# Gated infini-attention on one core: O weighed in 32-token blocks turned by VectorE, memory by quads of heads, products copied out of PSUM once

## The chip, the core and the metric

The kernel runs on one core of a Trainium2 chip. TensorE (PE in the profile) multiplies matrices into PSUM, which has eight banks of 128 x 512 floats. VectorE (DVE), ScalarE (ACT) and GpSimd (POOL) work on tiles of 128 partitions; GpSimd reads and writes SBUF only. SyncE (SP) issues every DMA. The metric is device time in microseconds (us); the kernel before has a median of 1042.45 us over 3 runs (1041.78 to 1042.59).

## The reference

There are two branches, A and B, each with its own weights, on the same x of 2048 tokens by 640 features. Each has 32 heads of 20 features and goes through 4 segments of 512 tokens in turn. In a segment, with S the causal softmax and g = sigmoid(beta) per head:

```python
a_dot = softmax(q @ k.T * scale + mask) @ v
a_mem = (phi(q) @ M) / (phi(q) @ z + 1e-6)      # phi(t) = t + 1 if t > 0 else exp(t)
o     = g * a_mem + (1 - g) * a_dot
M, z  = M + phi(k).T @ v, z + phi(k).sum()      # memory, carried to the next segment
```

A branch's output is o @ wo, and the result is s * A + (1 - s) * B with s = sigmoid(x . gate_w) per token. Everything is float32.

## The kernel before

The work is laid out by a planner in Python: the function keeps a clock of its own for every engine (queues `A`, `D`, `G` and `S` for ScalarE, VectorE, GpSimd and SyncE), gives each operation an estimated cost, and emits the instructions in the order in which its clock reaches them. Each engine then runs its own list in that fixed order, and waits on semaphores. The costs, the table `RULES` and the priorities therefore set the order on every engine, and a changed cost anywhere moves instructions everywhere.

There are 8 stages `t` (4 segments, A and B in turn), and in each 8 units `u` of 4 heads (a quad), so 64 units `i = 8 t + u`. TensorE's array is used as two halves of 64 rows, called lanes here, that run side by side; only PV (below) takes the whole array, in four column strips.

- Products (`job_qk`, `job_v`, `job_o`, line 643): x @ wq, wk, wv and O @ wo. Each operand is split into a high and a low part (fp32r), and three products are added, 15 matmuls of 512 columns in each lane. The products are the fill that keeps TensorE occupied between the units' steps.
- A finished q or k product is read out of its PSUM bank by `hi_lo_out` (ScalarE makes the high part, line 628, VectorE the low one, line 612) and by `hi_lo_phi` (lines 595 to 606), which makes phi; the bank is free when all have read it. High and low parts go to DRAM (`qd`, `kd`) and come back as quads (`qst`, `kst`, line 1032).
- S (line 1074) computes scores for the row maxima, which VectorE takes (line 1061, two instructions each); T (line 1164) computes the transposed scores, ScalarE the exponentials (line 1156), GpSimd the causal mask (line 1157).
- PV (line 1184) multiplies with v, which lies in `vst`, one tile for each branch, with a column of ones per head for the sum. Its result has 32 partitions per head (20 values, the sum, 11 that are not used) and 512 tokens.
- `fin_unit`: the result is copied out (line 1209), turned back to tokens on partitions by 8 matmuls with the identity (`turn`, line 790), weighed by VectorE (lines 1248 to 1250) into `ft` or O, and added to O by GpSimd (line 1259).
- `mem_unit` (line 752) multiplies phi(q) with the memory `mbd` into tokens on partitions, for 19 or 13 heads at a time, and VectorE weighs it into O (lines 766 to 769). `back_unit` and `update_unit` (lines 790, 830, 851) renew the memory.
- `o_transpose` turns O once more (8 matmuls, line 790), and ScalarE and VectorE split it (line 1277) for the product with wo.

## Time and profile before

| | before |
|---|---|
| median of 3 runs | 1042.45 us |
| the profiled execution's span, first to last instruction | 1041.1 us (no other time of this execution is given; the median is 1.3 us more) |
| TensorE busy, instructions | 1031.4 us (99%), 11778 |
| VectorE busy | 759.5 us (73%) |
| ScalarE busy | 663.7 us (64%) |
| GpSimd busy | 583.9 us (56%) |
| DMA, mean share of 16 engines | 65% |
| granted TensorE clock | 1.00 |

Busy time is the union of the instructions' spans. A matmul's span holds its way through the array too, so that matmuls overlap and the distance between two starts says what one of them costs. A float32 matmul stands in the trace as two matmuls, each with its weight load (PEld); an fp32r matmul or a turn with the identity stands as one.

### The profile page before, as it was taken

The page shows a single profiled execution, that of the slowest core. Times are in us where ns is not written, and L with a number is a line of the kernel's source. Part 1 is how long each engine was busy: PE and PEld are TensorE (multiplying, and loading weights), DVE is VectorE, ACT ScalarE, POOL GpSimd, SP SyncE. Part 2 cuts the span into 40 slices and gives each one's busy share as a digit, 9 for nine tenths or more (in the row PEclk, how much of TensorE's full clock was granted, in tenths as well). Part 3 has the DMA queues.
Part 4 walks back from the last instruction along what each step waited for, and adds up shares of the span by engine and source line. Part 5 has one row for each costly group of instructions (what it writes and reads, how often), then busy time and mean ns, then how long its engine had stood idle before and what let it go on. Part 6 is the DMA issues. An engine that isn't in the chain of part 4 may idle for free.

```text
span 1041.1 us, 31911 instructions
## 1 busy us (share of the span) xinstructions
PE 1031.4 (99%) x11778; PEld 875.0 (84%) x11778; DVE 759.5 (73%) x2714; ACT 663.7 (64%) x1346; POOL 583.9 (56%) x1045
## 2 busy tenths in 40 slices
PE   9999999999999999999999999999999999999998
PEld 7887798888988889887898988988879888787876
DVE  4797877668776688776877768877578767788763
ACT  6376667667664576565857558666675756766581
...
GB/s 270 309 277 166 204 244 221 189 176 258 150 229 130 199 267 181 223 160 160 271 154 227 129 215 251 200 212 155 203 250 156 256 157 195 265 159 225 127 118 52
DMA packets 110027, 207.96 MB, mean 200 GB/s; under 512 B 12464, under 2 KB 16560, under 8 KB 109872
## 3 DMA queue, kind: packets, MB, share of 16 engines
...
## 4 chain that ended last, share of the span: by engine, by line
PE 94%; DMA 3%; ACT 1%; DVE 1%; SPq 0%; POOL 0%; issue 0%; ACTq 0%; DVEq 0%
PE bank L643 54%; PE bank L1184 14%; PE bank L1164 7%; PE bank L1074 7%; PE bank L790 4%; PE bank L830 3%; PE bank L752 3%; DMA kst<-kd 1%; DMA row<-in_xT_dram 1%; DMA wst<-in_a_wk_dram 1%; PE bank L691 1%; PE bank L1099 0%; DMA qd<-row 0%; PE bank L1003 0%; DVE row L988 0%
## 5 line engine op out<-in xcount | busy, mean ns | idle before, releaser
L1061 DVE CUSTOM_DVE_ANT_0 bank<-bank,tri 128x384 f32<-128x384 f32 (+3 forms) x1024 | 474.8, 518 | 163.3 <-PE bank L1074 137.6
L643 PE MATMUL bank<-row,wh 64*128 64x512 f32 x2308 | 518.4, 404 | 0.3
L1156 ACT ACTIVATE p<-bank 128x512 f32<-128x512 f32 x598 | 328.6, 599 | 143.2 <-PE bank L1164 104.9
L1157 POOL TENSOR_SCALAR_AFFINE_SELECT p<-p 128x256 f32<-128x256 f32 (+1 forms) x598 | 214.3, 367 | 264.2 <-ACT p L1156 251.6
L643 PEld LDWEIGHTS bank<-row,wh 64*128 64x128 f32 x2308 | 322.9, 185 | 14.6 <-issue 1.8
L643 PE MATMUL bank<-row,wl 64*128 64x512 f32 x1154 | 302.4, 400 | 0.0
L472 POOL TENSOR_TENSOR wl<-wst,wh 128x640 fp32r<-128x640 f32 x115 | 181.6, 1582 | 46.5 <-ACT wh L470 46.0
L643 PE MATMUL bank<-wvh,row 64*128 64x320 f32 x1280 | 192.7, 318 | 0.1
L643 PEld LDWEIGHTS bank<-row,wl 64*128 64x128 f32 x1154 | 173.6, 185 | 6.4 <-issue 1.4
L1074 PE MATMUL bank<-kst,qst 60*128 60x128 f32 (+3 forms) x1024 | 176.9, 320 | 2.0 <-DMA kst<-kd 1.3
L1164 PE MATMUL bank<-qst,kst 62*128 62x128 f32 (+3 forms) x1024 | 174.6, 318 | 0.0
L643 PEld LDWEIGHTS bank<-wvh,row 64*128 64x128 f32 x1280 | 153.4, 185 | 3.1 <-issue 1.6
L1184 PE MATMUL bank<-p,vst 128*32 128x512 f32 (+3 forms) x1948 | 145.3, 431 | 0.0
L1061 DVE DVE_READ_ACCUMULATOR2_ANT mx<- 128x1 f32 x1024 | 143.3, 140 | 0.0
L1164 PEld LDWEIGHTS bank<-qst,kst 62*128 62x128 f32 x1024 | 126.9, 186 | 8.8 <-issue 1.4
L1074 PEld LDWEIGHTS bank<-kst,qst 60*128 60x128 f32 x1024 | 125.3, 185 | 10.6 <-issue 3.0
L1184 PEld LDWEIGHTS bank<-p,vst 128*32 128x32 f32 x1948 | 58.3, 109 | 85.6 <-issue 63.6
L643 PE MATMUL bank<-wvl,row 64*128 64x320 f32 x640 | 107.9, 312 | 0.0
L470 ACT CAST wh<-wst 128x640 fp32r<-128x640 f32 x119 | 86.5, 736 | 19.0 <-PE bank L643 13.0
L1209 ACT COPY row<-bank 128x512 f32<-128x512 f32 x62 | 36.5, 588 | 79.0 <-PE bank L1184 74.4
L643 PEld LDWEIGHTS bank<-wvl,row 64*128 64x128 f32 x640 | 85.6, 185 | 0.4 <-issue 0.4
L790 PE MATMUL bank<-ident,row 64*128 64x64 f32 x752 | 75.4, 225 | 0.5 <-DVE mx L1061 0.2
...
## 6 DMA issues: line engine op xcount, KB each, us to landing
qd<-row SPq DMA_DIRECT2D x120, 256.0 KB
kd<-row SPq DMA_DIRECT2D x120, 256.0 KB
qst<-qd SPq DMA_DIRECT2D x128, 240.0 KB
kst<-kd SPq DMA_DIRECT2D x128, 240.0 KB
...
```

What stands on the lines that cost most here:

```text
L470: put("A", 0.66, lambda: nc.scalar.copy(wh, w3), lambda: put(lo_eng, lo_cost, lambda: lo.tensor_tensor(out=wl, in0=w3, in1=r32(wh), op=ALU ...
L472: lambda: lo.tensor_tensor(out=wl, in0=w3, in1=r32(wh), op=ALU.subtract), end, prio=3), prio=6)
L643: return nc.tensor.matmul(bank_of, lhsT=w[ROWS[half]], rhs=x_[ROWS[half]], start=start, stop=stop)
L752: return nc.tensor.matmul(pm[:, a - h0:c - h0, :].rearrange("p h e -> p (h e)"), lhsT=r32(pqTs[t, m][ROWS[half], P * n:P * (n + 1)]), rhs= ...
L790: return nc.tensor.transpose(px[:, n, r], block(n)[r], ident[r, r])
L1061: put("D", w / 960.0 + 0.112, lambda: nc.vector.tensor_tensor_reduce(out=sc[:, off:off + w], in0=sc[:, off:off + w], in1=tri[:, L - w:], s ...
L1074: lane_ops[half].append((w * 0.000458, lambda pair=pair, qb=qb, off=off, w=w, r=r, sc=sc: nc.tensor.matmul(sc[:, off:off + w], lhsT=q[r, p ...
L1156: put("A", 0.49, lambda: nc.scalar.activation(pt, sc, AF.Exp, scale=SCALE), lambda: (bank.give(sc), put("G", 0.05 + 0.16 * len(todo), lamb ...
L1157: "G", 0.05 + 0.16 * len(todo), lambda: nc.gpsimd.affine_select(out=blocks, in_=blocks, pattern=[[0, len(todo)], [1, P]], base=0, channel_ ...
L1164: lane_ops[half].append((w * 0.000458, lambda pair=pair, kb=kb, off=off, w=w, r=r, sc=sc: nc.tensor.matmul(sc[:, off:off + w], lhsT=k[r, p ...
L1184: nc.tensor.matmul(po[32 * j:32 * j + 32, P * kb:], lhsT=vst[t % 2][:, kb, h * E1:h * E1 + 32], rhs=pts[i, n, f][0][:, off:off + w], start ...
L1209: either(0.52, lambda: nc.scalar.copy(r32(oT), po), 0.63, lambda: nc.vector.tensor_copy(r32(oT), po), end, 2)
```

## The change

- PV's result (and the memory's) is no longer turned on TensorE. VectorE turns it from its bank into a row in blocks of 32 x 32 (`weighed`, line 944 of the changed kernel): 32 tokens of a block come to lie on partitions, and each head keeps its group of 32 partitions, so that a partition holds a head's tokens in 16 blocks. The weights are worked out there (lines 862 to 866), and the row is scaled straight into O's tile (`scale`, line 888), or scaled in place and then added (`scale_own`, `add`, lines 891 and 896), by VectorE or GpSimd, whichever the planner's cost prefers, with 0.6 us put on VectorE's side.
- O's tiles `Z[t, k]` hold 32 features of a head group; `o_turn` (line 962) turns each back by VectorE. The features thereby come in another order, and wo's rows are put in that order at the start by `relay`: 13 DMAs for each branch within DRAM, in three steps (`nat`, `lin`, `wop`, lines 480, 473, 468). The loads of wo read `wop`.
- `mem_unit` takes a quad at a time with the memory as the stationary operand and phi(q) as the moving one, 512 columns wide (line 837), in place of the pieces of 84, 63 and 21 columns. `mall`, one tile for each branch, replaces `mbds`.
- A q or k product is copied out of its bank once (line 749, ScalarE or VectorE), and the bank is free; high, low and phi are made from the row in SBUF (lines 675, 692, 701 to 718), the low part by VectorE or GpSimd.
- One `vst` serves both branches, and `job_v` waits for the PV and the updates of the stage before. The rows that are shared (`NBIG`) go from 27 to 42.
- The token gates are spread to the new layout (line 621, 64 copies of 32 x 4), the planner's cost model has other costs, and `RULES` other numbers.

```diff
--- before.py
+++ after.py
-        0: "TSTSTSTSTS 1.010 2.38 0.30 8",
-        2: "TTSTSTSTSS 1.023 2.38 0.30 8",
...
+        0: "TSTSTSTSTS 1.036 3.71 0.31 6",
+        1: "TSTSTSTSTS 1.0 2.38 0.33 6",
+        2: "TSTSTSTSTS 1.0 2.38 0.36 6",
...
-    DONE = {"A": 0.14, "D": 0.11, "G": 0.1, "S": 0.0}
+    DONE = {"A": 0.14, "D": 0.12, "G": 0.1, "S": 0.0}
+    SEEN, MAX_DONE = 0.127, 0.06
...
-        e = min(ways, key=lambda e: load[e] + ways[e][0])
+        e = min(ways, key=lambda e: load[e] + ways[e][0] + 0.6 * (e == "D"))
...
-    mbds = [[const.tile([P, HI[m] - LO[m] + 1, E1], F32, name=f"mbd{b}_{m}") for m in range(KT)] for b in range(2)]
+    mall = [const.tile([P, H, 32], F32, name=f"mall{b}") for b in range(2)]
...
-    vst = [const.tile([P, NB, H * E1 + 12], F32, name=f"vst{i}") for i in range(2)]
+    vst = const.tile([P, NB, H * E1 + 12], F32, name="vst")
...
+    nat = [dram.tile([D, D], F32, name=f"nat{b}") for b in range(2)]
+    lin = [dram.tile([4, 8 * DH, D], F32, name=f"lin{b}") for b in range(2)]
+    wop = [dram.tile([P, KT, D], F32, name=f"wop{b}") for b in range(2)]
-    NBIG, NWST, NWH, SPARE = 27, 4, 4, 2
+    NBIG, NWST, NWH, SPARE = 42, 4, 4, 2
...
+    def relay(b):
...
+        def third(j):
+            dma(1.2, lambda: nc.sync.dma_start(
+                out=wop[b][32 * j:32 * j + 32], in_=lin[b][j].rearrange("(k q) c -> q k c", k=KT)), last, prio=RELAY[b])
+        def second():
+            for j in range(4):
+                dma(1.2, lambda j=j: nc.sync.dma_start(
+                    out=lin[b][j].rearrange("(u e) c -> u e c", e=DH),
+                    in_=nat[b].rearrange("(u j e) c -> j u e c", u=8, j=4)[j]), lambda j=j: third(j), prio=RELAY[b])
+        last = then_all(4, there)
+        first = then_all(KT, second)
+        for m in range(KT):
+            dma(1.2, lambda m=m: nc.sync.dma_start(
+                out=nat[b][:, P * m:P * (m + 1)].rearrange("(k p) c -> p k c", p=P), in_=weights[b]["o"][m]), first, prio=RELAY[b])
+    RELAY = (150.0, 260.0)
...
+            def fetch():
+                src_ = src[m] if kind in "qk" else wop[t % 2][:, :, P * m:P * (m + 1)]
+                dma(0.84, lambda: nc.sync.dma_start(out=w3, in_=src_), landed, prio=0 if i < 4 else need[i])
...
-            put("D", 0.63, lambda: nc.vector.tensor_tensor(out=lo, in0=src, in1=r32(hi), op=ALU.subtract), out, prio=1)
+            anyof(1, out, D=(0.65, lambda: nc.vector.tensor_tensor(out=lo, in0=r32(raw), in1=r32(hi), op=ALU.subtract)),
+                  G=(1.255, lambda: nc.gpsimd.tensor_tensor(out=lo, in0=r32(raw), in1=r32(hi), op=ALU.subtract)))
...
+    def phi_out(raw, y, read):
+        def end():
+            big.give(raw)
+            read[1](y)
+        def least():
+            put("D", 0.35, lambda: nc.vector.tensor_scalar(raw, raw, 0.0, 1.0, op0=ALU.max, op1=ALU.add), lambda: put(
+                "D", 0.65, lambda: nc.vector.tensor_tensor(out=y, in0=raw, in1=y, op=ALU.min), end, prio=1), prio=1)
+        def most():
+            put("D", 0.65, lambda: nc.vector.scalar_tensor_tensor(
+                out=y, in0=raw, scalar=0.0, in1=y, op0=ALU.max, op1=ALU.add), end, prio=1)
+        def summed():
+            put("D", 0.35, lambda: nc.vector.tensor_scalar(raw, raw, 0.0, None, op0=ALU.max), lambda: put(
+                "G", 1.255, lambda: nc.gpsimd.tensor_tensor(out=y, in0=raw, in1=y, op=ALU.add), end, prio=1), prio=1)
+        if load["D"] < load["A"]:
+            both = then_all(2, least)
+            put("A", 0.535, lambda: nc.scalar.activation(y, raw, AF.Exp), both, prio=2)
+        else:
+            both = then_all(2, summed if load["G"] + 0.9 < load["D"] else most)
+            put("A", 0.535, lambda: nc.scalar.activation(y, raw, AF.Relu, scale=-1.0), lambda: put(
+                "A", 0.535, lambda: nc.scalar.activation(y, y, AF.Exp, scale=-1.0), both, prio=2), prio=2)
+        read[0].append(both)
...
+            big.want((F32,), lambda raw: either(
+                0.478, lambda: nc.scalar.copy(raw, pp), 0.6, lambda: nc.vector.tensor_copy(raw, pp), lambda: out(raw), 1), prio=1)
...
+    def mem_unit(t, u):
+        w = mall[t % 2][:, 4 * u:4 * u + 4, :].rearrange("p h e -> p (h e)")
+        half_m = [next(c // 2 for c in CHUNKS[u] if c % 2 == half) for half in range(2)]
+        def mm(half, start, stop):
+            r = ROWS[half]
+            return nc.tensor.matmul(b, lhsT=w[r], rhs=r32(pqTs[t, half_m[half]][r, :]), start=start, stop=stop)
+        ops = [[(cost_f(L), lambda z0, z1, half=half: mm(half, z0, z1))] for half in range(2)]
...
+        def take():
+            read()
+            big.want((F32,), lambda z: weighed(t, u, b, z, 1), prio=1)
+        return split_unit(*ops, take)
+    def weighed(t, u, b, z, which):
+        z4 = z.rearrange("p (a e) -> p a e", e=32)
+        first = which == 1 or t < 2
+        def weight():
+            w = sb.tile([P, 16], F32, tag="fw", name=f"fw{which}_{t}_{u}", bufs=4)
+            if which:
+                nc.vector.scalar_tensor_tensor(
+                    out=w, in0=z4[:, :, DH], scalar=1e-6, in1=gq[t][1][:, u, :], op0=ALU.add, op1=ALU.mult)
+            else:
+                nc.vector.tensor_tensor(out=w, in0=z4[:, :, DH], in1=gq[t][0][:, u, :], op=ALU.mult)
+            nc.vector.reciprocal(w, w)
+            return w
...
+        def scale(e, w):
+            wb = w[:, :, None].to_broadcast([P, 16, DH])
+            for k, e0, e1 in ZP[u]:
+                dst = Z[t, k].rearrange("p (a e) -> p a e", e=32)[:, :, DH * u + e0 - 32 * k:DH * u + e1 - 32 * k]
+                e.tensor_tensor(out=dst, in0=z4[:, :, e0:e1], in1=wb[:, :, e0:e1], op=ALU.mult)
+        def scale_own(e, w):
+            e.tensor_tensor(out=z4[:, :, :DH], in0=z4[:, :, :DH], in1=w[:, :, None].to_broadcast([P, 16, DH]), op=ALU.mult)
+        def add(e):
+            for k, e0, e1 in ZP[u]:
+                dst = Z[t, k].rearrange("p (a e) -> p a e", e=32)[:, :, DH * u + e0 - 32 * k:DH * u + e1 - 32 * k]
+                e.tensor_tensor(out=dst, in0=dst, in1=z4[:, :, e0:e1], op=ALU.add)
...
+        n = len(ZP[u])
+        D1, G1 = 0.1 * n + 0.33, 0.14 * n + 0.69
+        def turned():
+            bank.give(b)
+            when_gates(lambda: put("D", 0.33, lambda: got_w.append(weight()), lambda: when_placed(go), prio=2))
...
+        def go():
+            w = got_w[0]
+            if first:
+                pair(D1, G1, lambda e: scale(e, w), end, 3)
+            else:
+                pair(0.43, 0.83, lambda e: scale_own(e, w), plus, 3)
+        def plus():
+            if (t, u) in mem_done:
+                pair(D1, G1, add, end, 3)
+            else:
+                at(clk[0] + 0.2, plus)
+        def pair(d, g, fn, then, prio):
+            anyof(prio, then, D=(d, lambda: fn(nc.vector)), G=(g, lambda: fn(nc.gpsimd)))
+        places(lambda: None)
+        put("D", 0.62, lambda: nc.vector.transpose(out=z, in_=b), turned, prio=2)
+    def o_turn(t, k, o):
+        def turned():
+            big.give(Z.pop((t, k)))
+            big.want((F32R, F32R), halves, prio=2)
+        def halves(hi, lo):
+            def end():
+                big.give(o)
+                OTs[t, k] = (hi, lo)
+            put("A", 0.535, lambda: nc.scalar.copy(hi, o), lambda: anyof(
+                2, end, **{x: (c, lambda e=e: e.tensor_tensor(out=lo, in0=o, in1=r32(hi), op=ALU.subtract))
+                           for x, c, e in (("D", 0.65, nc.vector), ("G", 1.255, nc.gpsimd))}), prio=2)
+        z = Z[t, k]
+        put("D", 0.6, lambda: nc.vector.transpose(out=o, in_=z), turned, prio=2)
...
-        yield from hold_on(lambda: t < 2 or oTs_begun[t - 2] == 8 and all((t - 2, m) in upd_done for m in range(KT)), "v")
+        ms = range(KT) if half else range(3)
+        yield from hold_on(lambda: t < 1 or oTs_begun[t - 1] >= 4 + 4 * half and (
+            t > 6 or all((t - 1, m) in upd_done for m in ms)), "v")
...
-    def fin_unit(i):
...
-        def weigh(dst):
-            w = sb.tile([P, NB, 4], F32, tag="fw", name=f"fw{i}", bufs=2)
-            wb = w[:, :, :, None].to_broadcast([P, NB, 4, DH])
-            nc.vector.tensor_tensor(out=w, in0=px[:, :, :, DH], in1=gq[t][0][:, :, 4 * u:4 * u + 4], op=ALU.mult)
-            nc.vector.reciprocal(w, w)
-            nc.vector.tensor_tensor(out=dst, in0=px[:, :, :, :DH], in1=wb, op=ALU.mult)
...
-    def o_transpose(t, k):
...
+        after_whole(lambda: (read(), big.want((F32,), lambda z: weighed(t, u, po, z, 0), prio=1)))
...
+        if (t, kind, m) == (0, "v", 4):
+            relay(0)
+        if (t, kind, m) == (1, "v", 0):
+            relay(1)
```

Three places show how instructions move. On TensorE, behind the PV of unit 27 (`row_8905_8142` is the copied PV result, `mt` the maxima), before:

```order
L1099 MATMUL bank_122<-ident,mt_8067 32x64
L790 MATMUL bank_121<-ident,row_8905_8142 128x64 x3
L643 MATMUL bank_123<-row_8310_7607,wh_135 128x512
L790 MATMUL bank_121<-ident,row_8905_8142 128x64
L643 MATMUL bank_124<-row_8156_7488,wh_129 128x512
L643 MATMUL bank_123<-row_8314_7610,wh_135 128x512
L643 MATMUL bank_124<-row_8305_7604,wh_129 128x512
L790 MATMUL bank_121<-ident,row_8905_8142 128x64 x2
```

and in the changed kernel behind the same PV:

```order
L1275 MATMUL bank_120<-ident,mt_7936 32x64
L734 MATMUL bank_118<-row_8641_7086,wl_128 128x512
L734 MATMUL bank_121<-row_8951_7381,wh_129 128x512
L734 MATMUL bank_118<-row_8682_7140,wl_128 128x512
L734 MATMUL bank_121<-row_8616_7055,wl_130 128x512
L1275 MATMUL bank_120<-ident,mt_7936 32x64
L734 MATMUL bank_118<-row_8804_7245,wl_128 128x512
L1250 MATMUL bank_116<-kst_78,qst_74 128x512
```

The turns with the identity (line 790) are gone, and products and the next S stand in their place. The memory of stage 2 on TensorE (`row` is phi(q)), before and then changed:

```order
L752 MATMUL bank_124<-mbd_0_70,row_4156_3815 128x84
L752 MATMUL bank_120<-mbd_0_70,row_4156_3815 128x84
L752 MATMUL bank_124<-mbd_1_71,row_4341_3960 128x84
L752 MATMUL bank_120<-mbd_1_71,row_4341_3960 128x84
L752 MATMUL bank_124<-mbd_2_72,row_4625_4184 128x84
L643 MATMUL bank_118<-wvh,row_3105_2827 128x320
```

```order
L837 MATMUL bank_120<-row_4601_3820,mall_70 128x512
L837 MATMUL bank_115<-row_4787_3955,mall_70 128x512
L734 MATMUL bank_116<-row_3384_2797,wh_133 128x512
L734 MATMUL bank_116<-row_3389_2800,wh_133 128x512
L837 MATMUL bank_115<-row_4787_3955,mall_70 128x512
L837 MATMUL bank_120<-row_4787_3955,mall_70 128x512
```

Many narrow matmuls with phi(q) as the weights become two wide ones for each quad, one in each lane. On VectorE, around the weighing of unit 23, before and then changed:

```order
L595 TENSOR_SCALAR bank_122<-bank_122 128x512
L1248 TENSOR_TENSOR fw_7123<-bank_121,gqd_140 128x16
L1249 RECIPROCAL fw_7123<-fw_7123 128x16
L1250 TENSOR_TENSOR ft_150<-bank_121,fw_7123 128x320
L596 TENSOR_TENSOR row_7733_7063<-bank_122,row_7733_7063 128x512
L1061 ISA bank_124,mx_7117<-bank_124,tri 128x512
```

```order
L709 TENSOR_SCALAR row_8237_6791<-row_8237_6791 128x512
L944 STREAM_TRANSPOSE row_8391_6900<-bank_121 128x512
L1237 ISA bank_115,mx_6869<-bank_115,tri 128x512
L1237 ISA mx_6869 128x1
L865 TENSOR_TENSOR fw_2_7_6917<-row_8391_6900,gqd_138 128x16
L866 RECIPROCAL fw_2_7_6917<-fw_2_7_6917 128x16
L1237 ISA bank_120,mx_6869<-bank_120,tri 128x512
L1237 ISA mx_6869 128x1
L891 TENSOR_TENSOR row_8391_6900<-row_8391_6900,fw_2_7_6917 128x16x20
L1237 ISA bank_115,mx_6869<-bank_115,tri 128x384
L1237 ISA mx_6869 128x1
L896 TENSOR_TENSOR row_6545_5419<-row_6545_5419,row_8391_6900 128x16x20
```

The weighing read a bank (lines 1248 to 1250); now a block turn reads it (line 944), and the weights, the scaling (line 891) and the addition to O (line 896, on GpSimd at line 1259 before) work on rows in SBUF, each with two operands there. In other units the planner gives the scaling or the addition to GpSimd. The maxima (line 1237, line 1061 before) stand between these steps. On SP, in stage 0 of the changed kernel (before, the rows of lines 480, 473 and 468 aren't there, and the others follow each other):

```order
L480 DMA nat_109<-in_a_wo_dram 128x5x128
L1208 DMA qst_74<-qd_89 60x2x512 x2
L1208 DMA kst_78<-kd_97 60x2x512 x2
L473 DMA lin_111<-nat_109 8x12800 x4
L1287 DMA qst_72<-mr_144 2x8x128 x2
L521 DMA wst_126<-in_b_wv_dram 128x640
L521 DMA wst_123<-in_b_wv_dram 128x640
L468 DMA wop_113<-lin_111 160x1x640 x3
L1208 DMA qst_75<-qd_89 60x2x512 x2
L689 DMA kd_98<-row_1895_1671 128x512 x2
```

The second step (line 473) waits until `nat` has landed, and the third (line 468) for `lin`; the loads of the next quads and the stores of `kd` stand behind them.

More of the change, by code (lines that the diff above doesn't have):

```diff
@@ L1201, in read @@
                         own_p.append(j)
-        def got(oT):
-            def end():
-                bank.give(po)
-                oTs[i] = oT
-                later(1, 0.44, lambda: fin_ok(i), lambda: fin_unit(i))
-            either(0.52, lambda: nc.scalar.copy(r32(oT), po), 0.63, lambda: nc.vector.tensor_copy(r32(oT), po), end, 2)
-        if i % 8 == 0 and t < 2:
-            Ot[t] = None
-            O_store.want(1, lambda o: Ot.__setitem__(t, o), prio=t)
-        after_whole(lambda: (read(), big.want((F32,), got, prio=1)))
```

450 lines of the change are left out of this document (212 added, 238 removed).

## The prediction

> **What bounds the kernel now.** I read the page's busy times first, then the chain of waits over the middle of the run (60 to 980 us), then who waits for whom.
>
> ```profile
> span 1041.1 us, 31911 instructions
> PE 1031.4 (99%) x11778; PEld 875.0 (84%) x11778; DVE 759.5 (73%) x2714; ACT 663.7 (64%) x1346; POOL 583.9 (56%) x1045
> ...
> by line: PE bank L643 57.9%; PE bank L1184 14.7%; PE bank L1074 7.8%; PE bank L1164 7.7%; PE bank L790 4.3%; PE bank L830 3.4%; PE bank L752 3.4%; PE bank L1099 0.5%; issue 0.2%; ACT p L1156 0.1%; DVE bank L1061 0.0%; DVE mx L1061 0.0%; ACT
> ...
> L1061 DVE CUSTOM_DVE_ANT_0 bank<-bank,tri 128x384 f32<-128x384 f32 (+3 forms) x1024 | 474.8, 518 | 163.3 <-PE bank L1074 137.6
> ```
>
> In those 920 us the chain lies on TensorE for 99.7%, and VectorE's longest wait is for TensorE (137.6 us). So TensorE's work sets the time, and a change is worth what it takes from TensorE's lanes, less what new lateness of others makes TensorE wait. How much lateness can be borne two stretches show:
>
> ```profile
> 60.00:70.00 10.00, 10.00 (x119) 8.01 (x119) 9.39 (x34) 8.73 (x20) 8.20 (x15) 1.00 0.97 341
> 120.00:130.00 10.00, 10.00 (x110) 7.95 (x110) 9.52 (x31) 7.32 (x16) 6.28 (x11) 1.00 0.49 165
> ```
>
> The columns are stretch, length, then busy time of PE, PEld, DVE, ACT, POOL, granted clock, DMA share and GB/s. VectorE is busy 94% and 95%, and TensorE still the whole 10 us.
>
> **TensorE: turns removed.** The order has 1072 turns with the identity before and 240 after: 832 go (512 of `fin_unit`, 320 of `o_transpose`).
>
> ```profile
> 60.00:980.00 920.00, 97.54 (x972) 83.04 (x972) 1.00 0.66 200
> ...
> 508.00 0.40 PE L790 MATMUL bank<-ident,row 64*128 64x64 f32 x4
> 508.20 0.39 PE L643 MATMUL bank<-row,wh 64*128 64x512 f32 x1
> 508.24 0.41 PE L790 MATMUL bank<-ident,row 64*128 64x64 f32 x4
> ```
>
> The first row is line 790 alone (972 of its matmuls). Bare, four turns take 0.24 us of one lane (508.00 to 508.24) while the other lane goes on: 0.03 us of both lanes each, 25 us for 832. By the chain it is 4.3% of 920 us over 972, so 40.7 ns, 34 us. The product behind a short turn has too little time to load its weights, and that loss stands on the product's line. So I fitted the 229 stretches of 4 us from 60 to 980 us by least squares: 4 us equals the sum over kinds of count times price. The first and the last of them, all engines and then line 790 alone:
>
> ```profile
> 60.00:64.00 4.00, 4.00 (x45) 3.84 (x45) 3.86 (x20) 3.51 (x8) 3.68 (x6) 1.00 0.96 331
> 976.00:980.00 4.00, 4.00 (x44) 4.00 (x42) 3.86 (x17) 3.72 (x7) 2.96 (x5) 1.00 0.37 108
> ...
> 60.00:64.00 4.00, 0.56 (x4) 0.37 (x4) 1.00 0.96 331
> 976.00:980.00 4.00, 0.00 (x0) 0.00 (x0) 1.00 0.37 108
> ```
>
> It prices a turn at 51.8 ns (standard error 2.5), a memory matmul at 60.1 (1.6). I take 50 ns, near the fit, since it is the price of having one more: **-41.6 us**, bounds -25 and -43.
>
> **TensorE: the memory.** 528 trace rows of line 752 go, at 3.4% of 920 us, 59 ns each: **-31.3 us**. In their place come 96 float32 matmuls of 512 columns, 48 in each lane. No such matmul in half the array is in the trace; the nearest are PV and the update:
>
> ```profile
> 1020.75 2.29 PE bank L1184 x32
> ...
> 60.00:980.00 920.00, 59.90 (x448) 51.34 (x448) 1.00 0.66 200
> ```
>
> PV's 32 rows run through 2 x 1280 columns in 2.29 us, 0.895 ns a column: 1024 columns for a float32 matmul of 512 are 0.916 us, and 48 of them 44.0 us. The update (line 830, second row) has 3.4% of 920 us for 448 rows of 151 columns on average in two lanes, 0.92 ns a column, which makes 45.3. The fit prices a product of 512 columns at 113.6 ns of both lanes, 0.227 of one; a float32 matmul of four such passes would be 0.909 us, 43.6 for 48. I take **+44 us**, bounds 43 and 46. The memory by itself thus costs 13 us more than before; only the turns gain.
>
> The remaining products, S, T, PV and updates are as many as before. v's matmuls stand in the same stretches between PVs as before, so the single `vst` adds no wait on TensorE. Sum on TensorE: -41.6 - 31.3 + 44 = **-28.9 us**.
>
> **VectorE and GpSimd: what comes on.** Spacing counts, not length: starts 505.09 and 505.69 make 0.60 us for a 512-wide operation.
>
> ```profile
> 505.09 0.69 DVE L595 TENSOR_SCALAR bank<-bank 128x512 f32<-128x512 f32 x1
> 505.69 0.69 DVE L1061 CUSTOM_DVE_ANT_0 bank<-bank,tri 128x512 f32<-128x512 f32 x1
> ...
> 509.95 0.17 DVE L1248 TENSOR_TENSOR fw<-bank,gqd 128x16 f32<-128x16 f32 x1
> 510.16 0.25 DVE L1249 RECIPROCAL fw<-fw 128x16 f32<-128x16 f32 x1
> 510.52 0.49 DVE L1250 TENSOR_TENSOR ft<-bank,fw 128x320 f32<-128x320 f32 x1
> 510.92 0.42 DVE L1061 CUSTOM_DVE_ANT_0 bank<-bank,tri 128x256 f32<-128x256 f32 x1
> ...
> L806 DVE COPY row<-bank 128x512 f32<-128x512 f32 x3 | 2.1, 686 | 3.0 <-PE bank L790 3.0
> L494 DVE TENSOR_TENSOR row<-row,row 128x512 fp32r<-128x512 f32 x5 | 3.3, 691 | 1.3 <-ACT row L490 1.3
> ...
> L1259 POOL TENSOR_TENSOR O<-O,ft 128x320 f32<-128x320 f32 x48 | 42.0, 876 | 43.2 <-DVE ft L1250 32.9 <-DVE mw L766 3.9 <-DMA kst<-kd 2.4
> L494 POOL TENSOR_TENSOR row<-row,row 128x512 fp32r<-128x512 f32 x15 | 19.3, 1288 | 1.2 <-ACT row L490 0.9
> ```
>
> Removed from VectorE: 216 512-wide operations (lines 612, 595, 596, 602, 1277) at 0.60, 130 us; 64 weighings at 0.97 (509.95 to 510.92), 62; 48 of the memory at about 0.9, 43: 235 us. Added: 152 block turns, which the trace lacks, at the 0.60 of a copy from a bank (bounds 0.60 and twice that), 91; 29 copies, 17; 127 operations with both operands in SBUF at 0.65 (line 494, 0.69 long), 83; 53 maxima with 0 (lines 701, 709) at 0.60, 32; 112 weights at 0.57, 64; 76 scalings and additions, 25; small copies, 6: 318. So 759.5 + 83 = 842 us, 83% of the new span. GpSimd gets 53 operations of 1.29 and 134 of at most 0.88 us in place of 48: +121, 705 us (70%). ScalarE changes by some -10. All lie beside TensorE.
>
> [...]
>
> **What is late next.** VectorE and GpSimd hold each other up when both of a VectorE operation's operands are in SBUF. Line 530 is the one such kind that recurs before:
>
> ```profile
> 28.32 1.15 DVE L530 CUSTOM_DVE_ANT_0 wst<-wst,gw 128x640 f32<-128x640 f32 x1 [1.59 <-issue]
> 29.61 1.97 DVE L530 CUSTOM_DVE_ANT_0 wst<-wst,gw 128x640 f32<-128x640 f32 x1
> ...
> 27.23 3.67 POOL L472 TENSOR_TENSOR wl<-wst,wh 128x640 fp32r<-128x640 f32 x2 [5.15 <-ACT wh L470]
> ...
> L530 DVE CUSTOM_DVE_ANT_0 wst<-wst,gw x16: 814/827/1966, 28.3 to 666.2; 128x640 f32<-128x640 f32 x16
> L530 DVE CUSTOM_DVE_ANT_0 wst<-wst,gw 128x640 f32<-128x640 f32 x16 | 15.1, 952 | 1.8 <-issue 1.6
> ...
> 133.72 2.11 POOL L472 TENSOR_TENSOR wl<-wst,wh 128x640 fp32r<-128x640 f32 x1 [4.31 <-ACT wh L470]
> ...
> L472 POOL TENSOR_TENSOR wl<-wst,wh 128x640 fp32r<-128x640 f32 x115 | 181.6, 1582 | 46.5 <-ACT wh L470 46.0
> ```
>
> It takes 0.81 us free, and 1.97 when it meets GpSimd's split, which is itself 2.11 instead of its 1.58 at 133.72. Mean less minimum is 952 - 814 = 138 ns. The change makes some 380 such operations (270 large, 112 weights): 138 ns each is 53 us. With GpSimd at 70%, 147 of its operations 1.58 us long, a random meeting costs about 0.23 us: 88 us. VectorE is then filled to 88-92%, not 83%. Its queue holds the maxima (line 1061), whose banks TensorE needs back; behind GpSimd's queue stand the masks that PV waits for. Eight banks and a lead of two units are the cover, and in the two stretches above it sufficed at 95%. I let about a tenth of 53 to 88 us through: **+7 us**, bounds 0 and half of 88, 44.
>
> [...]
>
> **DMA.** `relay` moves 1.6 MB three times for each branch. SP stands at line 473 until `nat` has landed and at line 468 until `lin` has, with the next quads' loads behind it.
>
> ```profile
> 80.00:90.00 10.00, 10.00 (x129) 8.40 (x125) 7.88 (x32) 4.56 (x10) 2.57 (x7) 1.00 0.68 184
> 90.00:100.00 10.00, 10.00 (x119) 8.62 (x113) 7.78 (x36) 7.97 (x16) 5.03 (x12) 1.00 0.33 97
> ```
>
> At about 280 GB/s when full, 4.9 MB are 17 us of all DMA engines, where these two stretches have 10 us free. Quads are loaded two units (some 32 us) ahead, so I take 0; without that cover it would be up to 10 us.
>
> **The end.** From PV's end (1023.04) to the last products before took 6.5 us; now a block turn, weights, two GpSimd operations and another turn take about 6. I take 0.
>
> **Sum.** 1041.1 - 28.9 + 7 = 1019.2 us of span; the median lies 1.3 above the span, so **1020.5 us**.
>
> **Rivals.**
> 1. *The turns were half hidden.* At the bare 0.03 us they give 25: 1041.1 - 25 - 31.3 + 44 + 7 + 1.3 = 1037. For it: the other lane goes on meanwhile. Against: chain and fit both price them higher.
> 2. *All lateness is covered.* 1041.1 - 43 - 31.3 + 43 + 1.3 = 1011. For it: the 95% stretches. Against: two engines fuller at once all along.
> 3. *VectorE and GpSimd in each other's way become the bound* (slower). If half of the 88 us reaches TensorE through banks not returned, and half of the 45 us or so by which GpSimd is held (15% of the time VectorE has the pair, 1000 operations, 0.3 us), it is 1013.5 + 44 + 22 = 1079 at most, and 1057 with VectorE's half alone. It decides from some 30 us let through. The same end is reached if a block turn takes twice a copy: 91 us more would fill VectorE.
> 4. *The relay delays quads*: 1030.
>
> **Chances.** Forecast 0.58 (own range 1012 to 1032), rival 1 0.08, rival 2 0.13, rival 3 0.16, rival 4 0.05. Range for 8 in 10: 1005, below rival 2 by the turn's and memory's errors, to 1047, a part of rival 3. A measurement of this kernel tells 0.2% (2 us) from no change. Faster 0.80, same 0.04, slower 0.16.
>
> **What would show it.** TensorE with 240 turns (line 968) in place of 1072, and its chain still above 98%; line 837 at 0.9 us between starts in a lane; line 944 near 0.69 us long; lines 675 and 702 with a mean well over their minimum. It would be wrong if TensorE shows long waits for VectorE's maxima or GpSimd's masks, or for `qst` and `kst` at 70 to 150 us.

## The result, and the profile after

The changed kernel takes 1111.62 us (median of 4 runs, 1110.32 to 1113.43), the kernel before 1042.12 on the same chip: 1.0676 times, with an interval of 1.0659 to 1.0694. It is 6.8% slower where 2.1% faster was forecast, and outside the stated range.

The page's first lines of the changed kernel:

```profile
span 1111.3 us, 29803 instructions
PE 1041.1 (94%) x10610; PEld 846.7 (76%) x10610; DVE 909.1 (82%) x2885; ACT 652.0 (59%) x1321; POOL 736.9 (66%) x1199
```

TensorE has 1168 matmuls fewer and yet is busy 9.7 us longer, and it is idle for 70.2 us (1111.3 - 1041.1), where it was idle for 9.7 before. The matmuls that were to go are gone; time came from somewhere else. Three places show where.

**The first 40 us.** Stretches of the changed kernel (stretch, length, busy time of PE, PEld, DVE, ACT, POOL, granted clock, DMA share, GB/s), and two rows of its SP queue (start, time, what it issues):

```profile
15.00:20.00 5.00, 4.94 (x38) 3.58 (x38) 0.00 (x0) 1.83 (x3) 2.10 (x2) 1.00 0.11 25
20.00:25.00 5.00, 3.29 (x30) 2.35 (x26) 0.27 (x2) 0.31 (x2) 0.00 (x0) 1.00 0.05 0
25.00:30.00 5.00, 0.00 (x0) 0.00 (x0) 0.00 (x0) 0.00 (x0) 0.00 (x0) 0.60 0.21 67
30.00:35.00 5.00, 0.00 (x0) 0.00 (x0) 2.35 (x5) 3.63 (x9) 0.99 (x2) 0.50 1.02 396
```
```profile
11.46 3.21 SPq L1557 DMA_DIRECT2D beta<-in_b_beta_dram  x4
...
19.30 5.75 SPq L547 DMA_DIRECT2D wst<-in_a_wq_dram  x1
```

From 15 to 25 us the DMA engines move next to nothing, SP stands 5.75 us at one load of wq, and then no engine has anything to do. Ahead in the queue are eight loads of `beta`, which the change made and which neither the diff shown above nor the prediction speaks of:

```diff
-    for b in range(2):
-        dma(0.9, ... out=bts[b], in_=betas[b].partition_broadcast(P))
+    for b in range(2):
+        for j in range(4):
+            dma(0.3, ... out=bts[b][32 * j:32 * j + 32],
+                in_=betas[b].rearrange("(u j) -> j u", j=4)[j].partition_broadcast(32))
```

Each takes every fourth number of beta, so 4 bytes at a time, 2048 pieces in all.

**VectorE held by GpSimd.** Groups of VectorE by shape in the changed kernel, then all of line 675 (shortest/median/longest, ns):

```profile
L944 DVE STREAM_TRANSPOSE row<-bank 128x512 f32<-128x512 f32 x112 | 77.9, 703 | 69.9 <-PE bank L1362 56.3 <-issue 9.4 <-PE bank L837 2.0
L675 DVE TENSOR_TENSOR row<-row,row 128x512 fp32r<-128x512 f32 x58 | 59.8, 1038 | 7.0 <-ACT row L692 7.0
L702 DVE TENSOR_TENSOR row<-row,row 128x512 f32<-128x512 f32 x50 | 52.1, 1053 | 0.5
L701 DVE TENSOR_SCALAR row<-row 128x512 f32<-128x512 f32 x50 | 32.2, 652 | 1.3 <-POOL row L676 0.3
L865 DVE TENSOR_TENSOR fw<-row,gqd 128x16 f32<-128x16 f32 x64 | 26.4, 413 | 0.8
...
L621 DVE COPY pgt<-pg 32x4 f32<-32x4 f32 x64 | 17.3, 270 | 0.9
```
```profile
L675 DVE TENSOR_TENSOR row<-row,row x58: 676/830/2053, 31.8 to 1028.8; 128x512 fp32r<-128x512 f32 x58
```

A low part (line 675) takes 0.68 us at its shortest and 1.04 on average. How it gets there can be seen at 764 us, on VectorE and then on GpSimd:

```profile
764.21 1.88 DVE L675 TENSOR_TENSOR row<-row,row 128x512 fp32r<-128x512 f32 x1
766.01 1.52 DVE L865 TENSOR_TENSOR fw<-row,gqd 128x16 f32<-128x16 f32 x1
767.57 0.25 DVE L866 RECIPROCAL fw<-fw 128x16 f32<-128x16 f32 x1
```
```profile
763.97 3.53 POOL L539 TENSOR_TENSOR wl<-wst,wh 128x640 fp32r<-128x640 f32 x2
```

GpSimd splits two weights in a row (line 539). VectorE's low part waits out the first, and a weight on 16 columns, 0.13 to 0.18 us when free, waits out the second and ends 0.03 us after it. The chain of waits runs through both:

```profile
764.29 1.80 DVE row L675
766.09 1.46 DVE fw L865
```

Over lines 675, 702, 701, 958, 862, 865, 891, 888, 896 and 604 the operations that began while GpSimd was at work, less the mean of those that didn't, make some 103 us (101 when the shapes of a line are kept apart, 113 when not).

**TensorE waits for VectorE's maxima, and then runs slowly.** TensorE's waits in the changed kernel (us in total, times, longest), and a stretch with such a wait:

```profile
PEld bank L1340 <- DVE mx L1237: 25.3, 24, 2.6
...
PE bank L1340 <- DVE mx L1237: 17.2, 17, 2.3
PEld bank L1250 <- DVE mx L1237: 17.1, 27, 1.6
```
```profile
465.00:470.00 5.00, 2.35 (x21) 1.83 (x20) 5.00 (x5) 0.17 (x1) 2.91 (x2) 0.98 0.96 315
470.00:475.00 5.00, 5.00 (x45) 4.74 (x45) 2.42 (x13) 1.13 (x3) 3.15 (x7) 0.68 0.40 111
```

Scores and transposed scores (lines 1250, 1340) lack a free bank, because the maxima that would free it stand behind held operations. After this gap, 2.65 us long (467.09 to 469.74), the granted clock is 0.68 for 5 us: 0.50 from 469.75 to 473.17, then 1.00. Seven of the 17 gaps over 1 us are followed by such a stretch, of 3.41 us in six cases and of 13.65 us behind the longest gap, of 11.98 us from 23.29 on. The trace has 34 us at half clock within the span, and TensorE is busy in 25 of them; a product of 512 columns (line 734) lasts 0.625 us there and 0.392 elsewhere (medians of 24 and 3456). Half of the 25, some 12 us, is my estimate of their cost; the kernel before has no such stretch and no gap over 1 us.

### The profile page after: what moved, and what is told of

Same layout as the page of the kernel before. It is cut to its first block, busy times and chain, and to the rows that moved or that the text cites. A ratio compares the mean times of both kernels' runs of the same rounds, so it can differ in the third digit from the quotient of the medians.

```text
span 1111.3 us, 29803 instructions
## 1 busy us (share of the span) xinstructions
PE 1041.1 (94%) x10610; PEld 846.7 (76%) x10610; DVE 909.1 (82%) x2885; ACT 652.0 (59%) x1321; POOL 736.9 (66%) x1199
## 2 busy tenths in 40 slices
DMA packets 140483, 217.63 MB, mean 196 GB/s; under 512 B 14704, under 2 KB 50800, under 8 KB 140272
## 5 line engine op out<-in xcount | busy, mean ns | idle before, releaser
L734 PE MATMUL bank<-row,wh 64*128 64x512 f32 x2308 | 537.2, 408 | 2.4 <-DVE mx L1237 2.2
L1237 DVE CUSTOM_DVE_ANT_0 bank<-bank,tri 128x128 f32<-128x128 f32 (+3 forms) x1024 | 473.2, 513 | 59.0 <-PE bank L1250 46.8
L1332 ACT ACTIVATE p<-bank 128x512 f32<-128x512 f32 x528 | 290.6, 599 | 179.9 <-PE bank L1340 141.1
L734 PE MATMUL bank<-row,wl 64*128 64x512 f32 x1154 | 315.4, 402 | 0.0
L734 PE MATMUL bank<-wvh,row 64*128 64x320 f32 x1280 | 210.2, 326 | 4.2 <-DVE row L944 3.3
L1340 PE MATMUL bank<-qst,kst 62*128 62x384 f32 (+3 forms) x1024 | 178.8, 325 | 21.1 <-DVE mx L1237 17.2
L1250 PE MATMUL bank<-kst,qst 60*128 60x384 f32 (+3 forms) x1024 | 184.1, 329 | 11.3 <-DVE mx L1237 8.7
L1340 PEld LDWEIGHTS bank<-qst,kst 62*128 62x128 f32 x1024 | 127.8, 187 | 40.9 <-DVE mx L1237 25.3
L1250 PEld LDWEIGHTS bank<-kst,qst 60*128 60x128 f32 x1024 | 129.8, 187 | 31.3 <-DVE mx L1237 17.1
L1362 PE MATMUL bank<-p,vst 128*32 128x256 f32 (+3 forms) x1788 | 138.8, 420 | 0.0
L944 DVE STREAM_TRANSPOSE row<-bank 128x512 f32<-128x512 f32 x112 | 77.9, 703 | 69.9 <-PE bank L1362 56.3
L837 PE MATMUL bank<-row,mall 64*128 64x512 f32 x192 | 83.7, 626 | 4.2 <-DVE row L702 1.6
```

The costliest lines, as they stand in the source:

```text
L734: return nc.tensor.matmul(bank_of, lhsT=w[ROWS[half]], rhs=x_[ROWS[half]], start=start, stop=stop)
L837: return nc.tensor.matmul(b, lhsT=w[r], rhs=r32(pqTs[t, half_m[half]][r, :]), start=start, stop=stop)
L944: put("D", 0.62, lambda: nc.vector.transpose(out=z, in_=b), turned, prio=2)
L1237: put("D", w / 960.0 + 0.112, lambda: nc.vector.tensor_tensor_reduce(out=sc[:, off:off + w], in0=sc[:, off:off + w], in1=tri[:, L - w:], s ...
L1250: lane_ops[half].append((cost_r(w), lambda pair=pair, qb=qb, off=off, w=w, r=r, sc=sc: nc.tensor.matmul(sc[:, off:off + w], lhsT=q[r, pair ...
L1332: put("A", 0.493, lambda: nc.scalar.activation(pt, sc, AF.Exp, scale=SCALE), lambda: (bank.give(sc), put("G", 0.137 + 0.118 * len(todo), l ...
```

## The experiments

My theory after the traces: the small pieces of beta cost the head some 15 us; the meetings of VectorE and GpSimd hold VectorE for 100 us, and nearly all of this reaches TensorE. Rivals: VectorE has too much to do in any case; the order is laid out with wrong lengths; products, banks or DMAs are late for another reason. Times are medians, ratios stand against the kernel before on the same chip.

| run | us | ratio (95%) | VectorE busy |
|---|---|---|---|
| change | 1111.6 | 1.068 (1.066 to 1.069) | 909 |
| e1, beta contiguous | 1097.9 | 1.054 (1.052 to 1.057) | 911 |
| e2, e1 + GpSimd's weight splits only write | 1038.3 | 0.997 (0.995 to 1.000) | 844 |
| e9, e2 with its wait kept | 1035.0 | 0.993 (0.991 to 0.995) | 838 |
| e8, e9 + masks, 512-wide only write | 1026.6 | 0.986 (0.984 to 0.987) | 823 |
| e11, e8 + 7 spreading copies | 1020.2 | 0.980 (0.978 to 0.982) | 817 |
| e13, e1 + 7 spreading copies | 1089.2 | 1.047 (1.044 to 1.049) | 903 |
| e10, e1 + splits in pieces | 1097.3 | 1.053 (1.051 to 1.056) | 881 |
| e12, e13 + low parts loaded | 1065.6 | 1.022 (1.018 to 1.026) | 851 |
| e3, e1 + products read from banks | 1068.1 | 1.026 (1.023 to 1.029) | 838 |
| e4, e1 laid out by real lengths | 1084.7 | 1.041 (1.037 to 1.045) | 877 |
| e5, e1 + splits once | 1084.3 | 1.041 (1.038 to 1.043) | 844 |
| e6, e3 + splits once | 1069.7 | 1.026 (1.024 to 1.028) | 814 |
| e7, e4 + splits once | 1071.4 | 1.028 (1.026 to 1.030) | 804 |
| b1, before + splits once | 1078.2 | 1.035 (1.032 to 1.038) | 760 |
| b2, before + memsets on VectorE | 1122.4 | 1.077 (1.074 to 1.080) | 840 |
| e14, e3 + spread, lengths, fitted table | 1028.7 | 0.988 (0.986 to 0.989) | 818 |
| e15, as e14 by the change's lengths | 1037.5 | 0.996 (0.995 to 0.998) | 836 |
| e16, e4 + spread, fitted table | 1057.2 | 1.015 (1.013 to 1.017) | 877 |

### Beta

```diff
-                out=bts[b][32 * j:32 * j + 32], in_=betas[b].rearrange("(u j) -> j u", j=4)[j].partition_broadcast(32))
+                out=btw[b], in_=betas[b].partition_broadcast(P))      # once for each b
+    nc.vector.tensor_copy(bts[b][32 * j:32 * j + 32], btw[b].rearrange("p (u j) -> p j u", j=4)[32 * j:32 * j + 32, j])
```

> The changed kernel with one edit: beta is loaded as before, two contiguous loads, and eight small VectorE copies put it where the changed kernel wants it; the order of everything else is untouched. Theory head: in the changed kernel TensorE stands idle 12 us from 23.3 us on while the DMA engines move almost nothing (0.11 and 0.05 of their time from 15 to 25 us) behind eight loads of beta, and its clock is then 0.5 to 0.6 until 40 us; with contiguous loads the idle time goes and the run ends 13 to 19 us earlier, 1093 to 1099. Rival: the wait is for wk's or wv's split, which other loads would delay all the same; then less than 4 us change, 1108 or more.

1097.87: 13.7 us less. The transfers under 512 bytes fall as the pieces go; the changed kernel's row, then this one's:

```profile
DMA packets 140483, 217.63 MB, mean 196 GB/s; under 512 B 14704, under 2 KB 50800, under 8 KB 140272
```
```profile
DMA packets 138595, 217.65 MB, mean 199 GB/s; under 512 B 12816, under 2 KB 48912, under 8 KB 138384
```

So the head's loss was beta, and 1888 small packets went with it (14704 - 12816). All runs from here on have this edit.

### Who holds VectorE

e2 keeps GpSimd busy in the same places, but lets it write where it read; the weights' low parts are left out but for 64 columns:

```diff
-  lo.tensor_tensor(out=wl, in0=w3, in1=r32(wh), op=ALU.subtract)
+  writes(wl)      # two memsets
+  lo.tensor_tensor(out=wl[:, :1, :64], in0=w3[:, :1, :64], in1=r32(wh[:, :1, :64]), op=ALU.subtract)
```

> As e1_betas, and GpSimd's splits of the weights (lines 514 and 539, 147 of 1.6 us) no longer read whole tiles: two memsets fill wl with zeros and a subtraction of 64 columns follows, about as long in sum. wl is left out but for those 64 columns. Theory exclusion: VectorE's operations with two operands in SBUF are held while GpSimd reads SBUF; without the long reads lines 675 and 702 fall from means of 1.04 and 1.05 us to about 0.8, line 865 from 0.41 to 0.25, VectorE's busy time by about 60 us, and the run ends 35 to 60 us before e1_betas. Rival load: VectorE is late by the number of its operations and their place in its queue; means fall or don't, but the time moves by less than 15 us. Second rival, GpSimd's own load: it is kept, so no change of time.

1038.32: 59.6 us less than e1, with VectorE busy 67 us less and GpSimd as long as before (727.7 against 738.6):

```profile
PE 1011.9 (98%) x10610; PEld 839.1 (81%) x10610; DVE 844.1 (82%) x2893; ACT 649.1 (63%) x1321; POOL 727.7 (70%) x1527
...
L675 DVE TENSOR_TENSOR row<-row,row 128x512 fp32r<-128x512 f32 x58 | 45.1, 784 | 8.9 <-ACT row L692 8.0 <-ACT mr L1292 0.6
L702 DVE TENSOR_TENSOR row<-row,row 128x512 f32<-128x512 f32 x50 | 36.7, 747 | 0.5
L701 DVE TENSOR_SCALAR row<-row 128x512 f32<-128x512 f32 x50 | 32.1, 653 | 1.4 <-POOL row L676 0.5
```

TensorE's waits for the maxima (PEld, lines 1340 and 1250), 25.3 and 17.1 us in the changed kernel, are 5.0 and 7.0. VectorE's number of operations and their order are those of e1, so the load isn't it. In e9 the subtraction stands ahead of the memsets, so that GpSimd's wait for ScalarE's cast stays in its place.

> As e2_writes, but the subtraction of 64 columns, which waits for ScalarE's cast, comes ahead of the two memsets, which fill all of wl with zeros; so GpSimd's queue waits for wh as long as in e1_betas. Theory exclusion: it is the reading that counts, so 1033 to 1045 as e2_writes. Rival: e2_writes gained because GpSimd waited less (47 us of waits for wh in the changed kernel) and its masks came earlier; then 1060 to 1090.

1034.95, so it isn't that wait either. e8 lets the masks (`affine_select`, which reads one operand) and GpSimd's 512-wide subtractions write only, too, so that the causal mask and most of those low parts are left out:

```diff
-  nc.gpsimd.affine_select(out=blocks, in_=blocks, ...)
+  nc.gpsimd.memset(blocks, 1.0)
```

> As e9_wait_kept, and GpSimd's masks (line 1333, 528) and its 512-wide subtractions (lines 676, 958) are memsets too (the masks are left out: ones stand in the diagonal blocks; of the low parts 64 columns are right). GpSimd reads SBUF in long operations hardly any more. The order is untouched. Theory exclusion, by its sum: of the 103 us by which VectorE's two-operand operations were lengthened (lines 675, 702, 701, 958, 862, 865, 891, 888, 896, 604, their mean beside a running GpSimd operation less that without one) 67 went in e2_writes with 60 us of time; the other 36 go with most of 30 more: VectorE's busy time 810 to 825 us, the time 1005 to 1020. Rival load: the rest of the loss is VectorE's larger work; 1030 or more.

1026.60, VectorE busy 823 us, and its two-operand operations are back at their own length (0.68 us free); line 701, with one operand, isn't quite (0.42 free):

```profile
L675 DVE TENSOR_TENSOR row<-row,row 128x512 fp32r<-128x512 f32 x58 | 40.0, 696 | 9.0 <-ACT row L692 5.5 <-DMA qst<-qd 1.8 <-POOL row L488 0.9
L702 DVE TENSOR_TENSOR row<-row,row 128x512 f32<-128x512 f32 x50 | 34.5, 703 | 0.5
L701 DVE TENSOR_SCALAR row<-row 128x512 f32<-128x512 f32 x50 | 25.2, 516 | 0.9
```

The time is 6.6 us above the range I expected. At 156, 405 and 664 us TensorE was idle beside VectorE's 16 small copies of the token gates (line 621), for which my working let nothing through to TensorE. e11 spreads them by 7 copies (4 into the first partition group, 3 from there), e13 does so with nothing left out:

> As e8_all_writes (masks and most of the low parts left out), and the token gates are spread over the four partition groups by 7 copies for each segment, not 16 (line 621). Theory all lateness counts: 36 copies of 0.27 us less are 10 us of VectorE, most of it in three runs of 4 us beside which TensorE stood idle; 1014 to 1020. Rival: those copies are gaps in VectorE's queue that cost nothing; 1024 to 1029.

> The changed kernel with beta loaded as in e1_betas and the token gates spread by 7 copies a segment, nothing left out. All lateness counts: 10 us under e1_betas, 1085 to 1091. Rival: no change, 1095 to 1100.

6.4 and 8.7 us less, so these copies counted nearly whole. From the change to e11 it is 13.7 + 71.3 + 6.4 = 91.4 us, and 1111.6 - 91.4 = 1020.2.

e10 shows that shorter instructions don't help, done in this way: GpSimd's weight splits and its 512-wide subtractions (lines 514, 539, 676, 958) in four pieces each. Line 568 stays whole.

> As e1_betas, with nothing left out and the order untouched: GpSimd's splits and 512-wide subtractions are done in four instructions of a quarter each (lines 514, 539, 676, 958; pieces of 160 or 128 columns). Theory exclusion: a held VectorE operation waits for the rest of one GpSimd instruction only, so for a piece of some 0.5 us, not one of 1.6; VectorE's busy time falls from 911 to 850 to 875 us and the time to 1040 to 1065, unless GpSimd, with perhaps 100 us more to do, becomes late itself. Rival: GpSimd's next piece follows on without letting VectorE in; 1090 or more.

1097.28, no gain. Its page, its GpSimd group, and GpSimd and VectorE at 189 us:

```profile
PE 1040.4 (95%) x10610; PEld 855.6 (78%) x10610; DVE 881.1 (80%) x2893; ACT 652.2 (59%) x1321; POOL 843.8 (77%) x1809
...
L539 POOL TENSOR_TENSOR wl<-wst,wh 128x160 fp32r<-128x160 f32 x460 | 258.5, 594 | 34.5 <-ACT wh L537 34.3
```
```profile
189.33 2.55 POOL L568 TENSOR_TENSOR row<-row,row 128x512 fp32r<-128x512 f32 x2
191.85 1.94 POOL L539 TENSOR_TENSOR wl<-wst,wh 128x160 fp32r<-128x160 f32 x4
193.75 0.53 POOL L1333 TENSOR_SCALAR_AFFINE_SELECT p<-p 128x128 f32<-128x128 f32 x2
```
```profile
189.64 5.19 DVE L675 TENSOR_TENSOR row<-row,row 128x512 fp32r<-128x512 f32 x1 [2.19 <-ACT row L692]
```

VectorE gets 30 us back and GpSimd has 105 more to do; eight instructions in a row (two whole ones of line 568, four pieces, two masks) held one low part for 5.19 us, to 0.55 us after the last of them, without letting it in between. That run doesn't tell how much of the missing gain is this and how much GpSimd's longer work.

### How much lateness passes

b2 asks this of the kernel before, where meetings hardly play a part: two memsets of VectorE ahead of each of 80 low parts.

> The kernel before, with two memsets of 512 columns on VectorE ahead of each of the 80 low parts of line 612, some 66 us more for VectorE, writing only; the order of everything is untouched. It asks how much lateness of VectorE such an order lets through to TensorE. My prediction took a tenth: 1045 to 1052. If e2_writes' rate (60 us of time for 67 of VectorE) holds for any order of this kind, whatever VectorE's share of busy time (73% here): 1085 to 1105. If the change used up the slack: 1045 or less.

```profile
PE 1063.0 (95%) x11778; PEld 886.2 (79%) x11778; DVE 839.5 (75%) x2874; ACT 665.5 (59%) x1346; POOL 584.5 (52%) x1045
...
L612 DVE MEMSET row<- 128x512 f32 x160 | 77.6, 485 | 18.0 <-DVE row L612 13.9
```

1122.39: 81 us more for 80 us of VectorE, which is then busy 75% of the time. A quarter of idle time absorbed nothing, with all the added work in one place, the path of the q and k products. The rates of four runs in a fixed order, time by VectorE's busy time: 59.6 / 67.0 = 0.89 (e2), 62.9 / 72.9 = 0.86 (e9), 71.3 / 88.6 = 0.80 (e8), 81 / 80 = 1.01 (b2). In e2, e9 and e8 a part of the time may be GpSimd's, which is held less there too. Two other runs in a fixed order lie far lower: e10, where GpSimd has more to do, has 0.6 / 30, and e12 below, where DMAs are added, 23.6 / 52.

### With nothing left out

e3 undoes one part, the copy out of the banks; e4 gives the layout the measured lengths.

```diff
-  either(0.478, copy by ScalarE, 0.6, copy by VectorE, lambda: out(raw), 1)      # e3: hi_lo_out, hi_lo_phi of the kernel before
-  D=(0.65, ... in0=r32(raw), in1=r32(hi))                                        # e4
+  D=(1.0, ... in0=r32(raw), in1=r32(hi))
```

> As e1_betas, with one part of the change undone: a q or k product is read from its bank by all its readers, as before (lines 595 to 628 of the kernel before), not copied out once. The order of all engines moves with it. Some 110 two-operand SBUF operations and 29 copies of VectorE give way to 216 - 40 operations with an operand in a bank, which no GpSimd operation held up before. Theory exclusion: VectorE's busy time falls to 830 to 860 us and the time to 1040 to 1065. Rival banks: banks are held longer and TensorE waits for them instead; 1085 to 1110, with waits of TensorE for lines of this part. Rival load: 1080 to 1095.

> As e1_betas; the layout of the order is given the lengths that the trace of the changed kernel shows for VectorE's two-operand operations (1.0 us in place of 0.65 for lines 675, 702 and 705, 0.58 for 0.35 in 701 and 709, 0.6 for 0.33 for the weights, 0.7 for 0.43 and 0.37 us more for scaling and adding); nothing else. Theory order: the order was laid out for a VectorE that is faster than the real one, so its queue is in a wrong order and that lateness costs TensorE; with real lengths 1060 to 1080. Rival capacity: VectorE and GpSimd have too much to do whatever the order; within 8 us of e1_betas.

1068.10 and 1084.66, gains of 29.8 and 13.2 us over e1, each 3 to 5 us above the range I expected. Both lay the order anew, with a table `RULES` whose numbers were not chosen for it. What that can cost is shown by b1, the kernel before with each weight split once, stored in DRAM and loaded later, where I expected no change:

> The kernel before, with its weights split once as in e5_once. It is bound by TensorE, whose work is unchanged, and its VectorE had few operations with two operands in SBUF: 1036 to 1043, no more than 0.4% faster. If it gains 15 us or more, the gain of e5_once isn't the end of the meetings that the change brought.

```profile
PE 1066.4 (99%) x11778; PEld 902.3 (84%) x11778; DVE 759.8 (70%) x2712; ACT 603.4 (56%) x1238; POOL 425.5 (39%) x935
```

37 us slower with less to do on GpSimd and ScalarE, VectorE unchanged and TensorE busy 99%: the same 11778 matmuls take longer as a whole, though one of 512 columns in a lane is as long as before (0.404 us, 0.403 before). They lie less well side by side: the time with only one or two in flight goes from 125 to 154 us. What part of it the added DMAs have, this run doesn't tell. The same edit added to e1, e3 and e4 (e5, e6, e7) gave 1084.3, 1069.7 and 1071.4, where I had expected 1025 to 1045, 1012 to 1035 and no gain over e5. VectorE is busy 844 us in e5, as in e2, and the time is 46 us longer: where the order moves, VectorE's busy time alone doesn't set the time, and these runs are no measure of the meetings. e12 keeps the order and loads only the low parts:

> As e13_betas_spread, with nothing left out and the order of all else untouched: 54 of GpSimd's splits are stored in DRAM, and 110 later ones aren't computed again but loaded, by a DMA that ScalarE issues behind its cast. GpSimd reads SBUF for 1.6 us 110 times less. Theory exclusion: as e2_writes, three quarters of its 60 us, and GpSimd is earlier too; VectorE's busy time about 850 us, 1035 to 1055. Rival DMA: the engines go from 65% to some 80% of their time, quads come late and TensorE waits for qst and kst; 1065 or more.

1065.61, 23.6 less than e13 for 52 us of VectorE: the meetings can be lifted with nothing left out, but at a rate of 0.45 and with a time above the range I expected. The added queue takes 10.6% of the DMA engines' time, and TensorE now waits for exponentials of ScalarE, which issues the added loads (5.8 us of weight loads of S, 1.4 in e13). That these take the rest back wasn't tested.

```profile
q10 hardware_dynamic: 16352, 34.41, 10.6%
```

Last, the table fitted anew (its numbers chosen so that the planner's own layout ends early), with products read from banks and longer lengths for weights, scaling and the split of O (e14), the same by the change's lengths (e15), and the copy out of the banks kept, by e4's lengths (e16):

> The changed kernel with beta loaded as in e1_betas, token gates spread as in e13_betas_spread, products read from their banks as in e3_psum, longer times given to the layout for weights, scaling and the split of O (0.6 for 0.33, 0.6 for 0.43, 0.27 us more, 0.9 for 0.65), and the numbers of RULES fitted anew to that. Nothing is left out. e3_psum took 1068; less 9 for the spread (e13 against e1) and the 25 us or so that an ill-fitting table costs (37 in b1_before_once, part of it DMA): 1025 to 1045. If turns and weighing by VectorE are themselves too much: 1055 or more.

> As e14_psum_fitted with the changed kernel's own lengths for weights, scaling and the split of O, and RULES fitted to those. VectorE is late by what they are held (some 40 us in the changed kernel), and lateness passes: 5 to 25 us over e14_psum_fitted. Rival: the table is all that counts; within 5 us of it.

> As e4_costs with the spread of e13_betas_spread and RULES fitted anew; the products are copied out once, as in the change. e4_costs took 1085; less 9 and some 25: 1045 to 1060, so not under the kernel before, since the meetings remain and differ from the mean that the layout counts with. If it comes under 1041, the change needed only true lengths.

```profile
PE 1014.9 (99%) x10610; PEld 846.8 (82%) x10610; DVE 818.1 (80%) x2782; ACT 628.2 (61%) x1287; POOL 700.7 (68%) x1225
```

e14 takes 1028.73 us, 0.9875 of the kernel before (0.9858 to 0.9891): faster than both kernels, with the block turns, the memory by quads and the single v tile of the change. VectorE is busy 818 us in it, 80%, so a load of that size isn't the bound. e15 is 8.7 us slower than e14, within what I expected if the time that VectorE is held costs more where the layout doesn't know of it; but the two tables differ too. e16 stays above the kernel before: of the two forms tried with a fitted table, only the one without the copy out of the banks, whose readers then have two operands in SBUF, gains.

## Why the prediction was wrong, step by step

- **TensorE, -28.9 us: right within what the runs tell.** 1168 matmuls left the trace. In e11, where little lateness is left (TensorE idle 1019.1 - 1005.7 = 13.4 us, 9.7 before), TensorE is busy 25.7 us less than before (1031.4) and the time is 1020.2; the sum without its 7 us of lateness was 1013.5. A float32 matmul of 512 columns in one lane, which stood in no trace before and which the prediction put at 0.909 to 0.916 us, is 0.86 us in the changed kernel: its two rows of line 837 start 0.429 us apart (318.237, 318.666, 319.094, 319.523). That e11 also comes so near to the forecast of 1020.5 is chance: it leaves out the masks, most low parts and with them most of the lateness.
- **Block turn, 0.60 us or up to twice that: right.** No run had shown one when 0.60 was taken, from the distance between a copy's starts; it was an estimate. In the changed kernel line 944 is 0.703 us long (0.702 beside GpSimd, 0.705 without), a copy from a bank (line 749) 0.684, and where the next operation doesn't wait, it starts 0.63 us after a block turn and 0.60 after such a copy (medians).
- **VectorE's 842 us, and 53 to 88 more by meetings: right in sum by luck.** 909 measured, but less 103 us of meetings it is 806. The meetings were more than taken, and the operations less: a maximum with 0 (line 701) takes 0.42 us when free, not 0.60, and a weight with its reciprocal 0.39 to 0.43, not 0.57.
- **"I let about a tenth of 53 to 88 us through: +7 us": this term failed.** The meetings took some 103 us. Of the 88.6 us of VectorE's time that e8 takes away, 71.3 come off the kernel's time, 0.80 and not a tenth; e2 and e9 have 0.89 and 0.86. TensorE's waits for VectorE's maxima, which the prediction named as a sign of being wrong, are there. I had read from two stretches with VectorE busy 94% and 95% and TensorE busy throughout that lateness is covered. But there VectorE was, as I now read it, busy and on time: the order had been laid out for that load. Slack would have had to be seen in how long results lie before they are used, and b2 shows that there is next to none. That the chain lay on TensorE for 99.7% says who came last at each step, not by how much.
- **Rival 3, 0.16, was the mechanism**, but with half of VectorE's lateness let through (1057, at most 1079 with GpSimd's). Without beta's pieces and most of the gates' copies the kernel still takes 1089.2 (e13). The 45 us that GpSimd was to lose it did lose: its split takes 1.61 us, 1.58 before, but its masks are longer too, some 27 us in 640 of them, and over all its groups, each operation less the tenth percentile of its group, it is 57 us, 9 before. The masks before and then changed:

```profile
L1157 POOL TENSOR_SCALAR_AFFINE_SELECT p<-p 128x256 f32<-128x256 f32 x376 | 149.5, 409 | 125.3 <-ACT p L1156 117.0
L1157 POOL TENSOR_SCALAR_AFFINE_SELECT p<-p 128x128 f32<-128x128 f32 x222 | 64.9, 298 | 138.9 <-ACT p L1156 134.6 <-ACT mr L1116 2.7 <-POOL p L1157 0.3
```
```profile
L1333 POOL TENSOR_SCALAR_AFFINE_SELECT p<-p 128x256 f32<-128x256 f32 x366 | 157.4, 444 | 70.3 <-ACT p L1332 65.3
L1333 POOL TENSOR_SCALAR_AFFINE_SELECT p<-p 128x128 f32<-128x128 f32 x162 | 54.8, 349 | 29.5 <-ACT p L1332 28.6
```

- **The head: a step that is missing.** Beta's eight loads, 13.7 us. The prediction went through what the shown diff says of DMAs, not through every DMA of the order. The relay, which it did go through, cost TensorE no wait for `qst` or `kst` that the trace shows, but one of 0.4 us.
- **The token gates' 64 copies: 6 us for all small copies on VectorE, and nothing on TensorE.** They are 17.3 us on VectorE, and 36 of them fewer gave 6 to 9 us.
- **The end, 0: about 5 us better.** The last PV is over at 1098.17 in the row below and the span ends 13.1 us later, 18.1 before.

```profile
1095.88 2.29 PE bank L1362 x32
```

What meets what, as far as the traces show it: VectorE's operations with two operands in SBUF meet GpSimd's reads and not its writes (line 675 takes 1.14 us on average in the changed kernel where GpSimd is at work when it begins or comes to work before it ends, and 0.685 where not; in e8 it takes 0.69 us beside memsets alone, and as much when GpSimd is idle). Where one of the two lies in a bank the kernel before shows no hold: line 612 takes 0.686 us beside GpSimd and 0.689 without. e8 changes masks and subtractions at once, but the changed kernel's trace parts them: beside masks alone, which read one operand, line 675 takes 0.81 us on average (5 operations). Line 701, with one operand in SBUF, is longer beside writes too: 0.56 us in e8 beside memsets alone and 0.42 free.

Open stays how much of b1's 37 us is DMA and how much the order, and what of e11's last 6.7 us (1020.2 against 1013.5) is still lateness. The relay, the single v tile and the quads are all in e11, so they have no more than that between them, unless TensorE's gain was larger than taken.
